# Two derivative tensors no longer stored, and the opening's x load, memsets and weight transposes moved in a four-layer forward and backward kernel

## The chip, the cores and the metric

The kernel runs on one core of a Trainium2 chip. The metric is the time of one execution in device microseconds (us); less is better.

## The reference

Input: x (2048 tokens of D = 640, bfloat16), the weights wqkv (640 x 1920) and wo (640 x 640) of a block A and of a block B, and grad_out. Four layers run, A, B, A, B, each with a residual:

```python
    x = x + _A_ref(_layernorm(x, axis=-1), A_wqkv, A_wo)
    x = x + _B_ref(_layernorm(x, axis=-1), B_wqkv, B_wo)
    x = x + _A_ref(_layernorm(x, axis=-1), A_wqkv, A_wo)
    x = x + _B_ref(_layernorm(x, axis=-1), B_wqkv, B_wo)
```

B is causal softmax attention in a window of 256 tokens, 32 heads of 20 elements. A is linear attention over all tokens with the same heads:

```python
    phi = lambda t: jnp.where(t > 0, t + 1, jnp.exp(t)) + 1e-6
    pq, pk = phi(q), phi(k)
    kv = jnp.einsum("bhsd,bhse->bhde", pk, v)
    z = jnp.einsum("bhsd->bhd", pk)
    num = jnp.einsum("bhqd,bhde->bhqe", pq, kv)
    den = jnp.einsum("bhqd,bhd->bhq", pq, z)[..., None] + 1e-6
    o = num / den
```

The kernel returns the last x and, from grad_out, the gradients of x and of the four weights. The backward pass of A needs the derivative of phi at q and at k: 1 where the argument is positive, exp(t) where it isn't, which is min(exp(t), 1). The kernel calls these eq and ek.

## The kernel before

**Tiles and stages.** The 2048 tokens are 16 tiles of 128 rows. The stages follow one another:

1. The opening (some 0 to 120 us): layer norm, q, k, v and phi of layer 0 for each tile; beside it the weights are loaded, constants are filled, and the transposed weights for the backward pass are made.
2. `a_kv(0)`: the sums over tokens of layer 0.
3. `ab_pass(0, False)`: tile by tile the end of layer 0, all of layer 1 (attention B), and layer norm with k, v of layer 2. The q work of layer 2 (`late_q`) follows, then `a_kv(2)` and `ab_pass(2, True)` (layers 2 and 3).
4. Backward: attention of layer 3, then a first pass over the tiles that ends layer 3 and does layer 2 (`lin_grads`, near 1240 to 1400 us), attention of layer 1, a second such pass (near 1960 to 2070 us), and a last part for layer 0's input.

**The opening, tile by tile.** `ln` has DVE make statistics (L476, L478), ACT form 1/sqrt (L479, L481), and DVE normalise into `hn` (L482); PE transposes `hn` (L464), ACT copies the result to `hnTA` (L467), and SP stores `hn` to DRAM for the backward pass. There is one buffer for `hn` here, so the next tile's L482 waits for PE's transposes and for this store. `a_qkv` then does six chunks of 320 columns, two for each of q, k and v, five matmuls each (L448). For q and k, ACT takes exp(t) into `ee` (L516), DVE cuts that at 1 (L517), which makes `ee` the derivative, and DVE forms phi = max(t, 1e-6) + `ee` (L520) into `pp` or `pk`. For v, ACT and DVE copy (L501, L504). phi(q) is transposed by PE and copied by ACT (`pqT`, L467). Five stores of 160 KB a tile leave on the ACT queue: pq, eq, pk, ek and v. `ee` has 4 buffers, `pp` 2.

**What stands beside it.**
- Layer 0's weight `Wqkv_A` comes in two loads on the ACT queue (chunks 0 and 1, then 2 to 5); x comes in three loads on SP (tile 0; tiles 1 to 3; tiles 4 to 15).
- `load_w`: fifteen row blocks of `Wo_A`, `Wqkv_B` and `Wo_B` on SP.
- `flip_w`: twenty times a DMA transpose of a 128 x 640 piece of a weight into one of two buffer rings (`KT`, `e`) and a DMA store of that to DRAM (`WqTB`, `WoTA`), all issued by SP. The backward passes read them.
- `zeros`: DVE memsets of `mbd`, the `qk_slab`s and the `v_slab`s (L1059), needed by later stages.
- `mask_steps`: small POOL operations.

**What sets the order.** A list scheduler (`Sched`) has each engine's instructions as operations with a planned duration, the keys they read and write, and a rank. `items` gives each piece a due time in tiles (4.5 is half a tile after tile 4 begins); the pieces are put in by due time, and `order()` then simulates the engines with the planned times and fixes each engine's own order. A key that the plan waits for, like `("rs", 0, 5)`, sets the planned place; the semaphores on the chip come from the data alone. A DMA's planned cost goes by its kind: "D" plain, "T" transposing, "B" a fixed time. On the chip SP issues its DMAs in its planned order, one behind the other: what stands behind a store that waits for its data waits too.

**The backward pass.** `lin_grads(tt)` in `start` loads for its tile, on SP, the transposed dN, pk and v, and eq and ek (two buffers each). `chunk` multiplies PE's result by eq or ek on DVE into `dqkv` (L1503). Around it in the same pass: POOL forms gw (L1327) and then, in the first pass, prod (L1377); DVE forms gcar from gw (L1329); ACT drains PE's result into dh (L1309).

Of the kernel before, what the change touches and what calls it, by code (L numbers as in the profile page):

```python
# [10 lines left out]
ACT = mybir.ActivationFunctionType  # L11
ALU = mybir.AluOpType
AX = mybir.AxisListType
BF = mybir.dt.bfloat16
# [72 lines left out]
class Sched:  # L87
# [38 lines left out]
    def order(self):  # L126
# [23 lines left out]
        while len(out) < len(self.ops):  # L150
# [16 lines left out]
            if o.dma:  # L167
                kind, size = o.dma
                if kind == "B":
                    free[e], chan_ = t + 1300, t + 2500  # L170
                elif kind == "T":
                    free[e] = t + 1100 + size / 1000
                    chan = max(chan, t + 800) + size / 140
                else:
                    free[e] = t + (330 if e == "SP" else 200)
                    chan = max(chan, t) + size / 300
                o.end = (chan_ if kind == "B" else chan) + 2000
            else:
                free[e] = t + o.dur
                o.end = free[e] + (170 if e == "PE" else 0)  # L180
# [22 lines left out]
class Kern:  # L203
    def __init__(self, ctx, tc, x0, A_wqkv, A_wo, B_wqkv, B_wo, grad_out, outs):
# [68 lines left out]
        for l in (0, 2):  # L273
            self.sv[l] = dict(
                pq=d.tile([T, D], BF, name=f"pq{l}"), pk=d.tile([T, D], BF, name=f"pk{l}"),
                eq=d.tile([T, D], BF, name=f"eq{l}"), ek=d.tile([T, D], BF, name=f"ek{l}"),
                v=d.tile([T, D], BF, name=f"v{l}"), o=d.tile([T, D], BF, name=f"o{l}"),
                r32=d.tile([T, self.H], F32, name=f"r32{l}"),
                mbd=d.tile([D, D + P], BF, name=f"mbd{l}"),
            )  # L280
# [53 lines left out]
    def forward(self, slabs):  # L334
# [5 lines left out]
        with ExitStack() as st:  # L340
# [130 lines left out]
            def ln(l, tt, hn, hnT, how):  # L471
# [13 lines left out]
                turn(how, lambda: hnT.t, lambda: hn.t, DT, [hn], [key_of(hnT)])  # L485
                dma("SP", lambda: self.tm_view(self.hn_d[l])[:, tt, :], lambda: hn.t, 160 * KB, [hn], [])

            def a_qkv(l, tt, hnT):
# [3 lines left out]
                def chunk(ci):  # L492
                    def f():
# [29 lines left out]
                        if ci == 3 and "q" in c:  # L523
                            p_, e = c["p"], c["q"]
                            turn("s", lambda: pqT[:, :, tt * P:(tt + 1) * P], lambda: p_.t, DT, [(p_, 0), (p_, 1)],
                                 [("pqT", tt)])
                            dma("ACT", lambda: self.tm_view(sv["pq"])[:, tt, :], lambda: p_.t, 160 * KB,
                                [(p_, 0), (p_, 1)], [])
                            dma("ACT", lambda e=e: self.tm_view(sv["eq"])[:, tt, :], lambda e=e: e.t, 160 * KB,
                                [(e, 0), (e, 1)], [])  # L530
                        if ci == 3:
                            e = c["k"]
                            dma("ACT", lambda: self.tm_view(sv["pk"])[:, tt, :], lambda: pk[:, tt, :], 160 * KB,
                                [("pk", tt, 2), ("pk", tt, 3)], [])
                            dma("ACT", lambda e=e: self.tm_view(sv["ek"])[:, tt, :], lambda e=e: e.t, 160 * KB,
                                [(e, 2), (e, 3)], [])
                    return f
# [4 lines left out]
            def late_q(l, tt, where="s1", **F):  # L542
# [25 lines left out]
                dma("ACT", lambda: self.tm_view(sv["pq"])[:, tt, :], lambda: p_.t, 160 * KB, [(p_, 0), (p_, 1)], [], **F)  # L568
                dma("ACT", lambda: self.tm_view(sv["eq"])[:, tt, :], lambda: e.t, 160 * KB, [(e, 0), (e, 1)], [], **F)

# [384 lines left out]
            for c0, c1 in ((0, 2), (2, 6)):  # L955
                dma("ACT", lambda c0=c0, c1=c1: wsb["Wqkv_A"][:, :, c0 * CW:c1 * CW],
                    lambda c0=c0, c1=c1: wA[:, :, c0 * CW:c1 * CW], 400 * (c1 - c0) * KB, [],
                    [("Wqkv_A", ci) for ci in range(c0, c1)])
            for t0, t1 in ((0, 1), (1, 4), (4, TT)):
                dma("SP", lambda t0=t0, t1=t1: x[:, t0:t1, :], lambda t0=t0, t1=t1: xin[:, t0:t1, :],  # L960
                    160 * (t1 - t0) * KB, [("Wqkv_A", 0)] if t0 == 4 else [], [("x", i) for i in range(t0, t1)])

# [21 lines left out]
            def ab_pass(l, last):  # L984
# [67 lines left out]
                else:  # L1052
# [3 lines left out]
            items = []  # L1056
            a_first(items, 0, 0)
            spread(items, 1.0, 9.0, [lambda f=f: op("POOL", 350, f, [], ["masks"]) for f in self.mask_steps])
            spread(items, 2.0, 12.0, [lambda t=t, v=v, n=n: op("DVE", 100 + n * 0.45, lambda: nc.vector.memset(t, v), [],  # L1059
                                                               ["zeros"]) for t, v, n in zeros])  # L1060
            for i, (k, src) in enumerate((("Wo_A", self.A_wo), ("Wqkv_B", self.B_wqkv), ("Wo_B", self.B_wo))):
                for j in range(DT):
                    tt = 1 + 3 * i + j
                    items.append((tt + 0.9, len(items), lambda k=k, src=src, j=j, tt=tt: load_w(k, src, "SP", j, [("vv", tt, 5)])))
            for i in range(4 * DT):
                at = 4.5 + 0.5 * i
                items.append((at, len(items), flip_w(i, ("rs", 0, int(at) - 1))))
            run(items)
# [22 lines left out]
    def bwd_phase(self, lb, la, nb, ahead, raw):  # L1091
# [9 lines left out]
        with ExitStack() as st:  # L1101
# [363 lines left out]
            def lin_grads(tt, items, t0):  # L1465
# [4 lines left out]
                def start():  # L1470
                    for nm, src, size in (("dNT", self.tmp_dN, 192 * KB), ("pkT", sv["pk"], 160 * KB),
# [3 lines left out]
                             [("dNd", tt)] if nm == "dNT" else [], [b])  # L1475
                    c["eq"], c["ek"] = load("eq", sv["eq"], tt), load("ek", sv["ek"], tt)

# [415 lines left out]
```

## Time and profile before

| | before |
|---|---|
| median of 3 runs | 2146.77 us (2145.37 to 2151.33) |
| the profiled execution | 2145.22 us |
| its span | 2143.5 us, so 1.7 us lie around it |
| mean granted TensorE clock | 0.975 |
| busy: PE, PEld, DVE, ACT, POOL | 2008.2, 1389.2, 1440.1, 1203.3, 879.4 us |
| DMA packets | 943687, 376.43 MB |
| eq stored from `ee` / ek stored from `ee` | 32 / 32 stores of 160 KB on the ACT queue |

PE is TensorE's matmuls, PEld its weight loads (they overlap), DVE VectorE, ACT ScalarE, POOL GpSimd, SP SyncE; SPq and ACTq are the DMA issues of an engine. A row of the list of groups names line, engine, operation, output <- inputs, shapes and count, then busy us and the mean ns of one, then idle time ahead of it and what ended that. In a timeline row stand the start, the duration, the instruction, and in brackets the idle time before it with its releaser. L-numbers are lines of the kernel before.

### The profile page before, as it was taken

To read this page: it belongs to the slowest core of one execution; us is meant where nothing else is said; L and a number is where in the kernel's file an instruction comes from. 1 tells how busy PE (TensorE), PEld (TensorE's weight loads), DVE (VectorE), ACT (ScalarE), POOL (GpSimd) and SP (SyncE) were. 2 spreads that over 40 slices of the span, in tenths; PEclk is the share of its full clock that TensorE was granted. 3 is DMA by queue.
4 is the path that set the end of the run, shared out by engine and by line. 5 is a ranking of instruction groups with operands and counts; after the bars stand their busy time and mean duration, and the time that the engine had idled before them with its cause. 6 is when DMAs were issued, how large, how long until landed. Compare 5 with 4: busy or idle time off the path is not lost. (4 is left out here: it accounts for less than half of the span.)

```text
span 2143.5 us, 68024 instructions
## 1 busy us (share of the span) xinstructions
PE 2008.2 (94%) x27908; PEld 1389.2 (65%) x27908; DVE 1440.1 (67%) x2954; ACT 1203.3 (56%) x1995; POOL 879.4 (41%) x1850
## 2 busy tenths in 40 slices
PE   6879999889999899999899999999999999999999
PEld 4656666656666577777666667656777765666764
DVE  6757777567776599999634368606998984444651
ACT  3527878647888589899422233216988881221430
POOL 1015666316777456666223223204665652230210
PEclk9989999999999899999899999999999999999999
DMA  9928989469998788987987899847999998989943
GB/s 291 256 106 179 191 193 191 119 198 201 210 208 191 146 157 151 161 161 155 193 185 168 213 200 203 175 104 142 157 158 151 170 170 162 199 185 227 186 111 102
DMA packets 943687, 376.43 MB, mean 176 GB/s; under 512 B 821776, under 2 KB 923664, under 8 KB 943120
## 3 DMA queue, kind: packets, MB, share of 16 engines
q1 hardware_dynamic: 866176, 299.16, 71.9%
q10 hardware_dynamic: 77200, 72.94, 11.1%
q8 instruction: 218, 3.57, 0.7%
q14 instruction: 93, 0.76, 0.1%
HBM read 109.02 MB, written 112.07 MB: 103 GB/s over the span
## 5 line engine op out<-in xcount | busy, mean ns | idle before, releaser
L1693 DVE TENSOR_TENSOR ds_sb<-pair,e_sb 128x768 bf16<-128x768 f32 x480 | 437.6, 951 | 57.8 <-PE pair L1654 49.6
L1673 ACT ACTIVATE e_sb<-pair 128x768 bf16<-128x768 f32 x480 | 390.9, 815 | 95.6 <-PE pair L1654 67.4
L839 POOL TENSOR_SCALAR_AFFINE_SELECT e_sb<-e_sb 128x384 bf16<-128x384 bf16 (+1 forms) x512 | 198.3, 406 | 357.5 <-ACT e_sb L830 335.7
L830 ACT ACTIVATE e_sb<-s_ps 128x1152 bf16<-128x1152 f32 (+2 forms) x256 | 273.8, 1070 | 100.2 <-PE s_ps L826 78.4
L1685 POOL TENSOR_SCALAR_AFFINE_SELECT e_sb<-e_sb 128x256 bf16<-128x256 bf16 x448 | 182.0, 406 | 227.1 <-ACT e_sb L1673 226.9
L1327 POOL TENSOR_TENSOR gw<-w,gcar 128x640 f32<-128x640 f32 x64 | 89.4, 1397 | 423.4 <-ACT w L1324 406.8
L1138 PEld LDWEIGHTS <-slabR 128*128 128x128 bf16 x1920 | 185.6, 98 | 116.1 <-DMA slabR<-o 3.7
L1682 POOL TENSOR_SCALAR_AFFINE_SELECT e_sb<-e_sb 128x256 bf16<-128x256 bf16 x512 | 206.5, 406 | 89.3 <-ACT e_sb L1673 89.3
L1718 PEld LDWEIGHTS <-dsT 128*128 128x128 bf16 x2880 | 146.2, 97 | 97.7 <-issue 91.5
L1709 ACT COPY dsT<-dsT_ps 128x768 bf16<-128x768 bf16 x240 | 191.2, 796 | 9.4 <-PE dsT_ps L1706 6.6
L448 PE MATMUL mm_ps<-slabR,hnTB 128*128 128x320 bf16 x960 | 170.5, 308 | 10.5 <-DVE gcar L520 6.0
L1706 PE MATMUL dsT_ps<-ident,ds_sb 128*128 128x128 bf16 x1848 | 158.2, 223 | 1.3 <-ACT dsT L1709 1.1
L1722 PEld LDWEIGHTS <-ds_sb 128*128 128x128 bf16 x2880 | 145.1, 96 | 0.8 <-issue 0.8
L1722 PEld LDWEIGHTS <-e_sb 128*128 128x128 bf16 x2880 | 145.0, 96 | 0.0
L844 POOL TENSOR_SCALAR_AFFINE_SELECT e_sb<-e_sb 128x512 bf16<-128x512 bf16 x224 | 142.6, 636 | 0.0
L833 ACT ACTIVATE e_sb<-s_ps 128x384 bf16<-128x384 f32 (+2 forms) x256 | 119.9, 468 | 32.3 <-PE s_ps L826 15.1
L1138 PE MATMUL dw_ps<-dqkv,slabR 128*128 128x480 bf16 x640 | 134.7, 366 | 0.0
L1309 ACT ACTIVATE dh<-mm_ps 128x320 f32<-128x320 f32 x64 | 28.0, 437 | 189.8 <-PE mm_ps L1138 164.9
L1138 PE MATMUL dw_ps<-dqkv,om 128*128 128x480 bf16 x640 | 134.2, 366 | 0.0
L1654 PE MATMUL pair<-slabR 32*128 32x384 bf16 (+2 forms) x1024 | 120.5, 326 | 12.0 <-DVE ds_sb L1693 5.2
L1138 PEld LDWEIGHTS <-om 128*128 128x128 bf16 x800 | 77.5, 98 | 71.3 <-DMA om<-o 2.4
L864 PEld LDWEIGHTS <-e_sb 128*128 128x128 bf16 x2880 | 105.5, 96 | 26.6 <-POOL e_sb L844 7.5
(234 smaller groups left out, 4357.6 us busy)
## 6 DMA issues: line engine op xcount, KB each, us to landing
qkvp<-qk_slab SPq DMA_DIRECT2D x64, 256.0 KB, 3.7
hn<-slabR SPq DMA_DIRECT2D x64, 160.0 KB, 2.9
qkvp<-v_slab SPq DMA_DIRECT2D x32, 256.0 KB, 3.4
slabR<-qkvp SPq DMA_DIRECT2D x16, 512.0 KB, 4.8
o<-o SPq DMA_DIRECT2D x48, 160.0 KB, 2.9
eq<-ee ACTq DMA_DIRECT2D x32, 160.0 KB, 3.0
pq<-pp ACTq DMA_DIRECT2D x32, 160.0 KB, 2.4
ek<-ee ACTq DMA_DIRECT2D x32, 160.0 KB, 2.7
```

Of the source, the lines that this page charges most:

```text
L448: nc.tensor.matmul(ps.t[:, w0:w0 + width], lhsT=lhsT(), rhs=rhs(), start=start, stop=stop)
L830: op("ACT", av(3 * nkt * P), lambda: nc.scalar.activation(e.t[:, 0:3, 0:nkt, :], s3.t[:, :, 0:nkt * P].rearrange("p h (i q) -> p h i q", q=P),
L839: nc.gpsimd.affine_select(out=v, in_=v, compare_op=ALU.is_ge, fill=0.0, base=0, pattern=[[0, h1 - h0], [1, P]], channel_multiplier=-1)
L1138: nc.tensor.matmul(ps.t[:, w0:w0 + width], lhsT=lhsT(), rhs=rhs(), start=start, stop=stop)
L1673: nc.scalar.activation(E[n][:, 2 * p:2 * p + 2], PR[h][:, :, 0:3 * P].rearrange("p i (j q) -> p i j q", q=P), ACT.Exp, scale=self.c_att)
L1682: nc.gpsimd.affine_select(out=e[:, :, j, :], in_=e[:, :, j, :], compare_op=ALU.is_ge, fill=0.0, base=0, pattern=[[0, 2], [-1, P]], channel ...
L1685: nc.gpsimd.affine_select(out=e[:, :, j, :], in_=e[:, :, j, :], compare_op=ALU.is_ge, fill=0.0, base=-1, pattern=[[0, 2], [1, P]], channel ...
L1693: nc.vector.tensor_mul(DS[n][:, hs], PR.pop(h)[:, :, 0:3 * P].rearrange("p i (j q) -> p i j q", q=P), E[n][:, hs])
L1706: nc.tensor.transpose(ps[:, i, j, :], DS[n][:, 2 * p + i, j, :], self.ident)
L1709: (nc.scalar.copy if by == "A" else nc.vector.tensor_copy)(TSB[h], TPS.pop(h))
L1718: nc.tensor.matmul(a[:, 0, hh, :], lhsT=TSB[2 * n + hh // 2][:, hh % 2, j, :], rhs=ld[g]["K"][:, k, cs], start=(i == 0), stop=(i == len(dq ...
L1722: nc.tensor.matmul(a[:, 1 + x, hh, :], lhsT=src[n][:, hh, j, :], rhs=ld[g][rhs][:, q, cs], start=(i == 0), stop=(i == len(dkv) - 1))
```

## The change

- **The derivative stores go.** The DRAM tensors eq and ek are gone, with their 64 stores: 32 in the opening (two a tile), 16 of ek in `ab_pass(0, False)`, 16 of eq in `late_q`. The backward pass loads pq and pk in their place and POOL forms min(phi - 1e-6, 1) in the buffer, 64 new operations of 128 x 640 bfloat16 with a planned 1000 ns.
- **The x load of tiles 4 to 15** comes at 0.5 and is planned behind tile 0's `hn` store (new key `("hnd", 0, 0)`); tile 0 and tiles 1 to 3 as before.
- **The fifteen weight loads** are keyed to the `hn` store of their tile instead of to the last copy of v of that tile.
- **The memsets** are spread from 3.0 to 13.0, each keyed to the statistics of tile 3 + 10 i / n, instead of from 2.0 to 12.0 without a key.
- **The twenty flips** are planned from 6.0 + 0.5 i instead of 4.5 + 0.5 i, each behind the statistics of the tile before.
- **The planner** gets a kind "L", with the landing time given, for the opening's large loads.

In each engine's order: SP issues the large x load right behind tile 0's `hn` store, then about one weight load a tile over tiles 1 to 14 (before: three a tile at the start); the first flip stands behind tile 4's `hn` store (before: tile 1's), the last behind tile 15's (before: tile 13's). On DVE the first large memset is the 24th instruction, and about one a tile follows to tile 13; before, they stood ahead of tile 0's statistics. The statistics and L482 of tile 1 now stand ahead of tile 0's L517. On POOL, in the steady part of the first backward pass, the order is eq's operation, gw, prod, ek's operation; in the second gw, ek's, eq's. PE has the same instructions; in `ab_pass(0, False)` a few transfers and exps change places.

```diff
+                if kind == "L":
+                    free[e], chan_ = t + 500, size - 2000
...
-                eq=d.tile([T, D], BF, name=f"eq{l}"), ek=d.tile([T, D], BF, name=f"ek{l}"),
...
-                dma("SP", lambda: self.tm_view(self.hn_d[l])[:, tt, :], lambda: hn.t, 160 * KB, [hn], [])
+                dma("SP", lambda: self.tm_view(self.hn_d[l])[:, tt, :], lambda: hn.t, 160 * KB, [hn], [("hnd", l, tt)])
...
-                            dma("ACT", lambda e=e: self.tm_view(sv["eq"])[:, tt, :], lambda e=e: e.t, 160 * KB,
-                                [(e, 0), (e, 1)], [])
...
-                            dma("ACT", lambda e=e: self.tm_view(sv["ek"])[:, tt, :], lambda e=e: e.t, 160 * KB,
-                                [(e, 2), (e, 3)], [])
...
-                dma("ACT", lambda: self.tm_view(sv["eq"])[:, tt, :], lambda: e.t, 160 * KB, [(e, 0), (e, 1)], [], **F)
...
-            for t0, t1 in ((0, 1), (1, 4), (4, TT)):
-                dma("SP", lambda t0=t0, t1=t1: x[:, t0:t1, :], lambda t0=t0, t1=t1: xin[:, t0:t1, :],
-                    160 * (t1 - t0) * KB, [("Wqkv_A", 0)] if t0 == 4 else [], [("x", i) for i in range(t0, t1)])
+                S.ops[-1].dma = ("L", 9500 if c0 else 5000)
+
+            def load_x(t0, t1, lands):
+                dma("SP", lambda: x[:, t0:t1, :], lambda: xin[:, t0:t1, :], 160 * (t1 - t0) * KB,
+                    [("hnd", 0, 0)] if t0 >= 4 else [], [("x", i) for i in range(t0, t1)])
+                S.ops[-1].dma = ("L", lands)
+            load_x(0, 1, 2800)
+            load_x(1, 4, 5500)
...
+            items.append((0.5, len(items), lambda: load_x(4, TT, 14000)))
...
-            spread(items, 2.0, 12.0, [lambda t=t, v=v, n=n: op("DVE", 100 + n * 0.45, lambda: nc.vector.memset(t, v), [],
-                                                               ["zeros"]) for t, v, n in zeros])
+            spread(items, 3.0, 13.0, [lambda t=t, v=v, n=n, i=i: op(
+                "DVE", 100 + n * 0.45, lambda: nc.vector.memset(t, v), [("rs", 0, 3 + i * 10 // len(zeros))], ["zeros"])
+                for i, (t, v, n) in enumerate(zeros)])
...
-                    items.append((tt + 0.9, len(items), lambda k=k, src=src, j=j, tt=tt: load_w(k, src, "SP", j, [("vv", tt, 5)])))
+                    items.append((tt + 0.9, len(items), lambda k=k, src=src, j=j, tt=tt: load_w(k, src, "SP", j, [("hnd", 0, tt)])))
...
-                at = 4.5 + 0.5 * i
-                items.append((at, len(items), flip_w(i, ("rs", 0, int(at) - 1))))
+                at = 6.0 + 0.5 * i
+                items.append((at, len(items), flip_w(i, ("rs", 0, min(int(at) - 1, TT - 1)))))
...
-                    c["eq"], c["ek"] = load("eq", sv["eq"], tt), load("ek", sv["ek"], tt)
+                    for nm, p_ in (("eq", "pq"), ("ek", "pk")):
+                        c[nm] = b = load(nm, sv[p_], tt)
+                        op("POOL", 1000, lambda b=b: nc.gpsimd.tensor_scalar(
+                            out=b.t, in0=b.t, scalar1=-1e-6, scalar2=1.0, op0=ALU.add, op1=ALU.min), [], [b])
```

## The prediction before the run

> **What bounds the kernel now.** First the page: the line of busy times, and the groups that price the new and the dropped work.
>
> ```profile
> span 2143.5 us, 68024 instructions
> ...
> PE 2008.2 (94%) x27908; PEld 1389.2 (65%) x27908; DVE 1440.1 (67%) x2954; ACT 1203.3 (56%) x1995; POOL 879.4 (41%) x1850
> ...
> q10 hardware_dynamic: 77200, 72.94, 11.1%
> ...
> L1327 POOL TENSOR_TENSOR gw<-w,gcar 128x640 f32<-128x640 f32 x64 | 89.4, 1397 | 423.4 <-ACT w L1324 406.8
> ...
> L844 POOL TENSOR_SCALAR_AFFINE_SELECT e_sb<-e_sb 128x512 bf16<-128x512 bf16 x224 | 142.6, 636 | 0.0
> ...
> eq<-ee ACTq DMA_DIRECT2D x32, 160.0 KB, 3.0
> ```
>
> PE is busy for 94% of the span, so 2143.5 - 2008.2 = 135 us are the most that an unchanged amount of PE work can give back. The view of busy time by stretches says where these lie (columns: stretch, length, busy us of PE, PEld, DVE, ACT, POOL, then granted clock, DMA share, GB/s).
>
> ```profile
> 0.00:25.00 25.00, 10.68 (x50) 6.37 (x51) 17.46 (x48) 6.88 (x16) 5.89 (x26) 0.88 0.94 316
> 25.00:50.00 25.00, 20.03 (x166) 14.02 (x165) 14.42 (x42) 11.75 (x30) 0.00 (x0) 0.91 0.97 279
> 50.00:75.00 25.00, 22.43 (x204) 16.43 (x203) 20.76 (x60) 16.15 (x39) 0.00 (x0) 1.00 0.90 246
> 75.00:100.00 25.00, 20.95 (x192) 15.30 (x191) 16.98 (x49) 14.68 (x38) 0.00 (x0) 1.00 1.05 263
> 100.00:125.00 25.00, 20.33 (x215) 15.37 (x213) 14.89 (x47) 9.94 (x23) 0.00 (x0) 1.00 0.63 195
> 300.00:400.00 100.00, 92.11 (x1647) 64.74 (x1645) 71.73 (x180) 81.83 (x133) 66.51 (x146) 1.00 0.83 178
> 2000.00:2020.00 20.00, 20.00 (x208) 15.85 (x206) 14.21 (x34) 8.46 (x23) 4.19 (x3) 1.00 0.84 188
> ```
>
> The first 100 us, the opening, hold 100 - (10.68 + 20.03 + 22.43 + 20.95) = 26 us of idle PE, with the DMA engines at 0.90 to 1.05. The forward pass has 8% idle beside an ACT at 82%; the last backward pass has none. So the opening is where this change can win much. Its waits (engine and line that waited <- engine and line that ended the wait: us in total, times, longest), the first row from 0 to 30 us, the others from 30 to 119:
>
> ```profile
> PE s_ps L464 <- DVE slabR L482: 13.5, 2, 9.8
> ```
>
> ```profile
> DVE ee L517 <- ACT ee L516: 17.5, 14, 3.1
> ...
> ACT hnTA L467 <- DVE pp L520: 6.2, 10, 1.2
> ...
> PE s_ps L448 <- ACT vv L501: 4.4, 7, 1.1
> ...
> PE s_ps L464 <- ACT ee L516: 3.4, 5, 1.0
> ```
>
> At first PE waits for the normalised tile (L482) of tiles 0 and 1. Later PE, DVE and ACT pass the wait round, and ACT is most often what the others wait for. The stores of the normalised tiles on SP mark the pace (start, duration):
>
> ```profile
> 20.08 0.33 SPq L416 DMA_DIRECT2D hn<-slabR  x1
> ...
> 42.50 0.33 SPq L416 DMA_DIRECT2D hn<-slabR  x1
> ...
> 50.15 0.35 SPq L416 DMA_DIRECT2D hn<-slabR  x1
> ...
> 109.62 0.34 SPq L416 DMA_DIRECT2D hn<-slabR  x1
> ```
>
> These are tiles 1, 4, 5 and 15: (42.50 - 20.08) / 3 = 7.5 us a tile early, and (109.62 - 50.15) / 10 = 5.95 us from tile 5 on.
>
> **Part 1: the memsets leave the head, the large loads move.** DVE before:
>
> ```profile
> 2.33 1.66 DVE L1059 MEMSET mbd<- 128x1920 uint32 x1 [0.35 <-issue]
> 4.04 1.57 DVE L1059 MEMSET qk_slab<- 128x512 uint32 x3
> 5.66 2.11 DVE L1059 MEMSET v_slab<- 128x512 uint32 x4
> 7.68 0.82 DVE L476 BATCH_NORM_STATS2 st<-x 128x6 f32<-128x320 bf16 x2
> ...
> 19.62 0.43 DVE L482 TENSOR_SCALAR slabR<-x,mv,rs 128x640 bf16<-128x640 bf16 x1
> ```
>
> Three groups, 1.66 + 1.57 + 2.11 = 5.3 us, stand ahead of tile 0's statistics at 7.68. In the changed order these follow the small constants, and the first large memset comes only as DVE's 24th instruction. Tile 0's x was asked for at 0.8, so its statistics can begin near 4, 3.7 us earlier. Tile 1's statistics and normalisation stand ahead of tile 0's phi work, so 19.62 can fall to about 11. PE can't use all of that, because the weights of chunks 2 to 5 must land:
>
> ```profile
> Wqkv_A<-in_A_wqkv_dram ACTq DMA_DIRECT2D x1, 1600.0 KB, 12.2
> x<-in_A_x_dram SPq DMA_DIRECT2D x1, 1920.0 KB, 15.4
> ```
>
> Asked for near 1 us and 12.2 us to landing, they arrive at 13 or 14; with the 1920 KB of x now queued behind tile 0's store, hence asked for at 6 rather than 3.4, perhaps a little earlier. From that point tile 1 follows without the gap. I take -4 us, between 0 (the loads decide) and -9 (all of 19.62 - 11). The memsets return at about one a tile, 5.3 us over ten tiles on a DVE that is busy for (20.76 + 16.98) / 50 = 75% there: nothing, +3 at most.
>
> **Part 2: 32 stores fewer in the opening.** Two things go: DMA work and ACT issue time. Queue 10 takes 11.1% of 2143.5 us for 72.94 MB, which is 0.53 us of all 16 engines for 160 KB, so 32 stores are 17 us. The five rows above from 0 to 125 us hold 25 x (0.94 + 0.97 + 0.90 + 1.05 + 0.63) = 112 us of DMA work; 95 stay. The issues, with tile 7 as the sample, and the place where ACT stood behind its own queue:
>
> ```profile
> 62.53 0.33 ACTq L416 DMA_DIRECT2D pq<-pp  x1
> ...
> 63.13 0.33 ACTq L416 DMA_DIRECT2D eq<-ee  x1
> ...
> 63.87 0.33 ACTq L416 DMA_DIRECT2D ek<-ee  x1
> ...
> 64.40 0.34 ACTq L416 DMA_DIRECT2D pk<-gcar  x1
> ...
> 65.05 0.34 ACTq L416 DMA_DIRECT2D v<-vv  x1
> ```
>
> ```profile
> 39.96 0.34 ACTq L416 DMA_DIRECT2D v<-vv  x1
> 40.35 0.44 ACT L516 ACTIVATE ee<-s_ps 128x320 bf16<-128x320 f32 x1 [2.18 <-DMA slabR<-in_B_wqkv_dram]
> ```
>
> Tiles 1 to 4: ACT's exp at 40.35 came 2.18 us late because the v store ahead of it waited for an earlier transfer, while the engines ran at 0.97. With 8 stores less (4 us of DMA work) and the 15 weight loads spread to a tile each, I take -4, between 0 (the other 1920 + 1600 KB still fill the engines) and -10 (three tiles at 5.4 instead of 7.5, and tile 4's extra wait).
>
> Tiles 5 to 15: ACT computes (16.15 + 14.68) / 50 = 62% of 5.95 = 3.7 us a tile and issues for 5 x 0.334 = 1.7, together 5.4 of 5.95. PE is busy for (22.43 + 20.95) / 50 = 87%, 5.2 us a tile, and can't go below that. Two issues less are 0.67; 5.95 - 0.67 = 5.28 is just above PE's floor. As DVE waits move into the gap, I take 0.5 a tile, 10 tiles, -5; the ends are 0 and -7.5 (PE's floor). What is late next is PE itself.
>
> The Trainium skill ("DMA: Bandwidth & Descriptors", Issuing engines are not separate DMA queues) says that an issue elsewhere saves only the sequencer's time, usually small beside the DMA. The rows agree on the size (0.33 beside 3.0 us to landing). By that rule the issue time would be worth nothing and these terms would shrink to the DMA work alone, which is the first rival's time.
>
> **Part 3: twenty flips from tile 6 on.** SP takes them in order between the stores of the normalised tiles: ten now stand among tiles 11 to 15. A flip's issue is 1 to 2 us of SP, two a tile with their stores 4 us, under the 5.4 of a tile. Nothing reads their result before the backward passes. I take 0, between -2 (early tiles freer) and +5 (one tile's pace at the end, if a late store holds the single hn buffer).
>
> **Part 4: behind the opening.** 16 ek stores leave the forward pass and 16 eq stores the q work behind it: 16 x 0.33 = 5 us of ACT issues where PE has 8% idle. Taken -2; ends -5 and +4 (the planner swaps a few transfers and exps there).
>
> **Part 5: 64 new POOL operations, 32 a pass.** None of this form (128x640 bf16 with one input) is in the trace; the nearest rows are L844 (0.64 for 512 columns, by width 0.80 for 640) and L1327 (1.40). I take 0.8. POOL is idle for most of a tile, so its time costs nothing by itself. The loads are issued a tile ahead; only the first tile may be some 0.4 late. But POOL and DVE collide. DVE, POOL, PE and ACT in the first backward pass:
>
> ```profile
> 1253.51 0.89 DVE L1329 SCALAR_TENSOR_TENSOR gcar<-slabR,sm,gw 128x640 bf16<-128x640 bf16 x1 [1.68 <-POOL gw L1327]
> 1258.85 1.95 DVE L1329 SCALAR_TENSOR_TENSOR gcar<-slabR,sm,gw 128x640 bf16<-128x640 bf16 x1 [0.35 <-POOL gw L1327]
> ```
>
> ```profile
> 1258.78 1.34 POOL L1377 TENSOR_TENSOR prod<-slab,o 128x640 f32<-128x640 bf16 x1
> ```
>
> ```profile
> 1297.85 0.44 ACT L1309 ACTIVATE dh<-dw_ps 128x320 f32<-128x320 f32 x1 [2.01 <-DVE dqkv L1503]
> ```
>
> ```profile
> 1298.43 0.42 PE L1145 MATMUL dw_ps<-slabA,pkT 128*128 128x320 bf16 x3 [0.27 <-ACT dh L1309]
> ```
>
> L1329 takes 0.89 alone and 1.95 when prod starts just before it. PE already waits 0.27 there for an ACT that waits for DVE, so DVE has no slack. The ek operation stands right behind prod on POOL. Does it hold DVE a second time? L1329 ended at 1260.80; less its own 0.89 it got going at 1259.91, 1.13 after prod began and 0.21 before prod ended. So DVE had come in before POOL's next instruction could, and I take +1 (first tiles) for the pass, with +20 as the far end. In the second pass the ek operation follows gw directly, where L1329 starts too; PE is at 20.00 of 20 and DVE at 14.21, so 0.6 a tile is covered: 0, at most +8.
>
> The Trainium skill ("GPSIMD Engine Reference", 1. Specifications) says that POOL shares its SBUF interfaces with VectorE and contends with DVE instructions of two SBUF inputs. The trace agrees (1.95 against 0.89), and the rule speaks against these 64 operations; by it the sum would be the last rival's.
>
> **Sum.** -4 - 4 - 5 + 0 - 2 + 1 = -14. The profiled run took 2145.22 us (its span and 1.7 around it), 1.6 under the median of the three; 2145.2 - 14 = 2131.
>
> **Rivals.**
> - *The opening is bound by what it moves or by PE, not by ACT.* For it: 0.90 to 1.05 DMA share, PE at 22.43 of 25. Against it: those shares include the dropped stores. Then only the head (-4) and half of the early tiles (-2) come: about 2139.
> - *The opening gives all its idle time.* Head -9, early tiles -9, later -7: with the rest about 2119. For it: 26 us of idle PE. Against it: the 12.2 us of the weights.
> - *Slower: the port in the first backward pass.* The ek operation gets the port ahead of the waiting L1329, in each steady tile, with no slack behind it. At 0.8 to 1.4 us for 14 tiles that is +11 to +20; with an opening that gives only 5 the time is 2151 to 2160, say 2155. It decides once the loss a tile passes gain / 14, 1 us by my sum. Against it: the 0.21 us just worked out.
> - *The change does nothing:* idle time goes to the next wait, 2145.
>
> **How the numbers follow.** Chances: forecast 0.53, first rival 0.18, all idle time 0.13, slower 0.09, nothing 0.07. Predicted: 2131. About 0.3% (6.4 us) is what a measurement of this kernel can tell from no change, so faster means under 2140.3. The forecast lies there nearly whole (0.51), the second rival whole, the first with more than half (0.11): 0.75. Within: 0.02 + 0.07 + 0.06 = 0.15, with 0.01 from the slower rival 0.16; slower 0.09. The range is 2112 to 2149: 2145 - 9 - 10 - 7.5 - 2 - 5 = 2112 is every term at its better end, and 2149 is the nothing case with part 4 at its worse end (+4); it leaves out the slower rival.
>
> **What would show it.** Right: tile 0's statistics near 4 us, tile 15's normalised store before 100 instead of at 109.62, 4.9 to 5.5 us a tile from tile 5 on, PE above 23 of 25 in the third stretch, L1329 still 1.95. Wrong: a store on SP held behind flips in tiles 11 to 15; L1329 at 2.7 or more; PE idle in the forward pass by what the opening gained.

## The result and the profile after

The changed kernel takes 2173.9 us (median of 4 runs, 2167.47 to 2174.88) beside 2146.07 us for the kernel before on the same chip: a ratio of 1.0124, 95% interval 1.0091 to 1.0156. It is 28 us slower. The forecast was 2131, and the range ended at 2149.

The page of the changed kernel, its line of busy times, the queue of the dropped stores, and the chain that ended last (by engine):

```profile
span 2173.2 us, 67954 instructions
...
PE 2019.4 (93%) x27908; PEld 1392.1 (64%) x27908; DVE 1440.3 (66%) x2954; ACT 1204.2 (55%) x1995; POOL 1041.4 (48%) x1914
...
q10 hardware_dynamic: 67984, 62.45, 9.3%
...
PE 5%; POOL 2%; DMA 1%; issue 1%; DVE 1%; SPq 0%; ACT 0%; ACTq 0%; POOLq 0%; DVEq 0%
```

The stores did go: queue 10 moves 62.45 MB instead of 72.94. But POOL is busy for 162 us more (1041.4 - 879.4), 2.5 us for each of the 64 new operations, and it stands in the last chain with 2%, where before it had 0%. The view of busy time by stretches, same columns and same stretches as before:

```profile
0.00:25.00 25.00, 13.45 (x82) 8.52 (x83) 13.81 (x38) 9.76 (x23) 6.01 (x26) 1.00 0.77 265
25.00:50.00 25.00, 23.45 (x208) 17.12 (x207) 20.71 (x61) 16.05 (x40) 0.00 (x0) 1.00 0.80 212
50.00:75.00 25.00, 20.15 (x193) 14.63 (x192) 19.41 (x59) 13.92 (x34) 0.00 (x0) 1.00 1.12 277
75.00:100.00 25.00, 20.68 (x173) 14.56 (x171) 16.24 (x49) 14.10 (x36) 0.00 (x0) 0.93 0.94 221
100.00:125.00 25.00, 18.18 (x183) 13.08 (x181) 13.70 (x42) 6.65 (x16) 0.00 (x0) 0.93 0.39 126
...
300.00:400.00 100.00, 91.44 (x1550) 62.48 (x1548) 70.06 (x173) 77.96 (x127) 62.81 (x139) 0.98 0.75 161
```

The first two stretches won 6.2 us of PE work (13.45 + 23.45 against 10.68 + 20.03), the third lost 2.3 (20.15 against 22.43), with the DMA engines at 1.12. The stores of the normalised tiles 1, 5 and 15 on SP (start, duration):

```profile
12.21 0.33 SPq L417 DMA_DIRECT2D hn<-slabR  x1
...
37.15 0.34 SPq L417 DMA_DIRECT2D hn<-slabR  x1
...
102.92 0.34 SPq L417 DMA_DIRECT2D hn<-slabR  x1
```

So the opening is 13.0 us ahead at tile 5 (50.15 before) and 6.7 at tile 15 (109.62). From then on the kernel falls behind. The starts of marked SP instructions in the profiled executions, with three runs explained further down, show where (us; the mbd store ends the opening, dNT is loaded once a tile in each backward pass):

| | before | after | drop_fused | drop_open | fused |
|---|---|---|---|---|---|
| hn store of tile 5 | 50.15 | 37.15 | 45.80 | 37.12 | 37.10 |
| mbd store | 121.63 | 116.25 | 113.40 | 113.65 | 115.81 |
| 24th hn store | 203.48 | 198.07 | 195.12 | 195.72 | 194.73 |
| 43rd hn store | 361.59 | 364.46 | 351.82 | 352.31 | 363.34 |
| 1st dNT load | 1083.73 | 1094.29 | 1075.96 | 1077.07 | 1088.27 |
| 16th dNT load (ends the first pass) | 1339.29 | 1355.23 | 1330.85 | 1335.23 | 1342.51 |
| 19th dNT load (second pass) | 1948.21 | 1967.91 | 1944.05 | 1944.65 | 1954.59 |
| 32nd dNT load | 2049.50 | 2077.02 | 2044.85 | 2045.82 | 2055.02 |

Against before, after is 5.4 us ahead at the mbd store and at the 24th hn store, 2.9 behind at the 43rd, 10.6 at the first dNT load, 15.9 at the 16th, 19.7 at the 19th and 27.5 at the last. Two places lose: the forward pass between the 24th and the 43rd store (8.3 us), and the backward passes. Most of the 7.7 us between the 43rd hn store and the first dNT load belongs to the backward side: the first of the new POOL operations stand there, from 1074.04 us on.

Theory P says that the backward loss is the POOL operations, by their length. Theory F says that the forward loss comes from the planner: without the stores in its account it writes another order. Rivals are late loads, the moved flips and weight loads, and the lighter ACT queue.

### The profile page after: what moved, and what is told of

Read it like the earlier page. It is cut to its first block, busy times and chain, and to the rows that moved or that the text cites. A ratio compares the mean times of both kernels' runs of the same rounds, so it can differ in the third digit from the quotient of the medians.

```text
span 2173.2 us, 67954 instructions
## 1 busy us (share of the span) xinstructions
PE 2019.4 (93%) x27908; PEld 1392.1 (64%) x27908; DVE 1440.3 (66%) x2954; ACT 1204.2 (55%) x1995; POOL 1041.4 (48%) x1914
## 3 DMA queue, kind: packets, MB, share of 16 engines
q10 hardware_dynamic: 67984, 62.45, 9.3%
## 5 line engine op out<-in xcount | busy, mean ns | idle before, releaser
L1329 POOL TENSOR_TENSOR gw<-w,gcar 128x640 f32<-128x640 f32 x64 | 89.4, 1397 | 227.8 <-ACT w L1326 214.3
L859 PE MATMUL pv_ps<-v_slab,e_sb 128*128 128x32 bf16 x2880 | 117.4, 177 | 9.3 <-POOL e_sb L839 8.3
```

The lines of the kernel that those rows point to most:

```text
L859: nc.tensor.matmul(pv.t[:, h % 16, :], lhsT=e.t[:, hh, j, :], rhs=vts[j].t[:, h, :], start=(j == 0), stop=(j == nkt - 1))
```

## The experiments

Where a run drops stores but says that the planner still counts them, each store is replaced by an operation that issues nothing and has the same planned cost:

```diff
-                            dma("ACT", lambda e=e: self.tm_view(sv["eq"])[:, tt, :], lambda e=e: e.t, 160 * KB,
-                                [(e, 0), (e, 1)], [])
+                            op("ACT", 60, lambda: None, [(e, 0), (e, 1)], [], dma=("D", 160 * KB))
```

The cut inside DVE's multiply, called the fused cut below, replaces the POOL operation:

```diff
-                            op("DVE", dve_ns(CW), lambda: nc.vector.tensor_mul(dst(), ps.t[:, 0:CW], e.t[:, e0:e0 + CW]),
+                            op("DVE", dve_ns(CW), lambda: nc.vector.scalar_tensor_tensor(
+                                out=dst(), in0=e.t[:, e0:e0 + CW], scalar=1.0, in1=ps.t[:, 0:CW], op0=ALU.min, op1=ALU.mult),
```

| run | stores | opening | order behind it | cut | median us | ratio to before (95%) |
|---|---|---|---|---|---|---|
| fused | dropped | new | new | fused | 2151.97 | 1.0032 (1.0014 to 1.0051) |
| drop_pool | dropped | old | old | POOL | 2158.65 | 1.0060 (1.0041 to 1.0079) |
| drop_fused | dropped | old | old | fused | 2134.78 | 0.9960 (0.9945 to 0.9975) |
| open_only | kept | new | old | none | 2148.77 | 1.0021 (1.0005 to 1.0036) |
| drop_open | dropped | new | old | fused | 2134.68 | 0.9946 (0.9931 to 0.9962) |
| drop_open_f45 | dropped | new, flips at 4.5 | old | fused | 2136.76 | 0.9965 (0.9952 to 0.9979) |
| drop_f60 | dropped | old, flips at 6.0 | old | fused | 2138.21 | 0.9972 (0.9956 to 0.9987) |
| drop_head | dropped | memsets and x new | old | fused | 2136.60 | 0.9962 (0.9947 to 0.9978) |
| forms | dropped | old | old | POOL, other forms | 2146.35 | 1.0003 (0.9987 to 1.0019) |
| drop_dve | dropped | new | old | DVE | 2134.02 | 0.9956 (0.9934 to 0.9979) |
| drop_f16 | dropped | new, flips at 16.0 | old | fused | 2140.24 | 0.9981 (0.9968 to 0.9994) |
| hidden | kept | new | new | none | 2176.00 | 1.0126 (1.0088 to 1.0163) |

The kernel before, measured beside each of these runs, had medians of 2144.79 to 2150.43 us, so a difference of 2 or 3 us between two rows is read from the ratios and their intervals.

**fused.** The changed kernel with the fused cut and without the POOL operations.

> The changed kernel without its 64 POOL operations: the cut min(phi, 1) is done inside DVE's existing multiply by the derivative (one instruction for one; the subtraction of 1e-6 is left out). Theory P (POOL): the operations, 2.35 to 3.04 us each in the trace, cost the 24 us that the backward passes lost (first tiles 7, first pass 8, second pass 9), so the time falls by 22 to 27 to 2147 to 2152, and the backward part is as long as before. Rival L (loads): the loads of pq and pk or the moved order of SP are late; then the backward part stays 15 us or more longer and the time is over 2160.

Measured 2151.97: 21.9 less than the changed kernel, as theory P said. In the table of marks, after minus fused is 6.0 us at the first dNT load, 12.7 at the 16th, 13.3 at the 19th and 22.0 at the last: the difference comes where the operations stand, 6 us at the first of them and the rest in the two passes. Rival L (late loads) falls, since the loads are the same here.

**drop_pool.** The kernel before without the stores, its order kept, with the POOL operations.

> The kernel before with the 64 stores dropped and the 64 POOL operations, but with the old opening and the old order of all engines in the forward pass (the planner still counts each dropped store, nothing is issued). Theory P: +24 in the backward part, 0 to -5 from the stores, so 2165 to 2171. Rival O (the opening's moves cost the time further on): 2142 to 2150.

2158.65, which is 23.9 over drop_fused: the operations' price once more, on another opening. It missed its expected range downwards because the stores are worth more than the 0 to 5 that I had put in.

**drop_fused.** The stores alone.

> The kernel before with the 64 stores dropped, every engine's order unchanged (the planner still counts them), and the cut at 1 inside DVE's multiply (without the subtraction of 1e-6): the stores alone. By the prediction's part 2 the opening's tiles go from 5.95 to 5.4 us and the early ones gain some 4, so -9 to -11 with part 4: 2135 to 2138. If stores hide behind other work: within 3 of 2146.

2134.78, 10.9 under the 2145.63 of before beside it. The marks are 8.2 us ahead at the mbd store and 9.8 at the 43rd hn store; 7.8 are left at the first dNT load and 4.7 at the last, in a profiled execution of 2140.33 us, above the run's median. Part 2 of the prediction (with 2 for part 4) had this size.

**open_only.** The opening's moves with all stores kept, and the old order behind.

> The changed kernel's opening (x load, memsets, weight loads, flips) with all 64 stores kept and the old backward pass; the order behind the opening is that of the kernel before. Theory F (the forward pass lost its 10 us because the planner, not seeing the stores, ordered its DMAs and exps otherwise): the opening's gain, 0 to 7, stays to the end, 2139 to 2146. Rival: the moved flips and loads cost it, and the forward pass is 5 to 10 longer here too, 2146 to 2156.

2148.77, 3 us slower than before, which misses theory F's range and lies in the rival's. But the place isn't the rival's: the mbd store comes at 126.4 instead of 121.63, and from there on the lag stays at 4.7 us to the 43rd hn store (366.33 against 361.59). So the order of before doesn't lose time in the forward pass, as theory F has it, and the new opening is no gain while the stores stand.

**drop_open.** drop_fused with the new opening; it differs from fused only in that the planner counts the stores.

> The stores alone (the run drop_fused) plus the whole changed opening; the planner still counts the dropped stores, so the order of every engine behind the opening is that of the kernel before. It differs from the run fused in the planner's view alone. Theory F (in fused the planner, not seeing the stores, put the forward pass in an order that lost 10 us): nothing is lost between tiles 7 and 16 of the forward pass, and the time is 2152 - 10 to 13 = 2139 to 2142. Rival C (a lighter ACT queue or the new opening slows the forward pass whatever the order): it is lost here too, 2150 to 2153.

2134.68, 17.3 under fused (18 by the ratios), beyond the 10 to 13 expected; rival C falls. The profiled executions show less of it: fused is 11.0 us later at the 43rd hn store and 9.5 at the end, but drop_open's was its slowest of ten, 2141.32. Busy time from 200 to 350 us, first of drop_open, then of fused:

```profile
200.00:350.00 150.00, 143.07 (x2483) 101.08 (x2482) 116.77 (x291) 124.18 (x201) 99.56 (x219) 1.00 0.88 181
```

```profile
200.00:350.00 150.00, 136.37 (x2292) 94.36 (x2290) 107.30 (x267) 113.62 (x187) 91.60 (x202) 0.99 0.81 168
```

PE does 6.7 us less in fused, with the lighter queue in both. What the new order waits for, by fused's list of waits for the same stretch (us in total, times, longest):

```profile
DVE qk_slab L690 <- PE mm_ps L449: 21.1, 19, 3.4
...
ACT e_sb L825 <- PE mm_ps L449: 15.5, 8, 2.3
```

The first kind of wait in drop_open's list:

```profile
DVE qk_slab L695 <- PE mm_ps L449: 7.3, 17, 0.9
```

ACT in the changed kernel, which has the new order too:

```profile
261.53 1.13 ACT L825 ACTIVATE e_sb<-s_ps 128x1152 bf16<-128x1152 f32 x1 [2.30 <-PE mm_ps L449]
...
278.75 1.13 ACT L825 ACTIVATE e_sb<-s_ps 128x1152 bf16<-128x1152 f32 x1 [1.83 <-PE mm_ps L449]
```

About once a tile ACT's exp now stands idle for some 2 us until a projection of PE has ended; drop_open's list has none of this kind among its twelve largest. In that order SP transposes `oTB` four instructions earlier, PE starts more of the q, k, v chunks in halves with scores between them, DVE's copies and norm steps shift with them, and ACT issues the `o` and `linv` stores ahead of an exp. So more changes in each tile than the few transfers and exps of the section on the change. Which of these swaps costs most wasn't tried.

**hidden.** The crossing's fourth corner: stores issued, planner not told.

```diff
+                            S.ops[-1].dma, S.ops[-1].dur = None, 0
```

(behind each of the eq and ek stores of open_only.)

> The other half of the crossing: the changed opening with all 64 stores issued and the old backward pass (the run open_only), but the planner is not told of the eq and ek stores, so PE, DVE, POOL and SP have the order of the run fused. Order and stores are then crossed: order of before and stores dropped 2134.7, order of before and stores issued 2148.8, new order and stores dropped 2152.0. Theory F (the new order costs 17 by itself): 2160 to 2168, and PE is busy for some 136 to 138 of the 150 us from 200 to 350, as in fused. Rival C (only the lighter ACT queue under that order loses time; with the stores issued it is harmless): 2146 to 2152.

2176.00, 27 over open_only, but before had 2150.43 beside it and 2145.63 beside open_only; by the two ratios it is 1.0126 - 1.0021, 22 us. In the profiled executions 3.6 us of it are there at the 24th hn store and 20.3 at the 43rd. Its own row from 200 to 350 us:

```profile
200.00:350.00 150.00, 135.85 (x2216) 91.76 (x2213) 104.24 (x260) 110.89 (x180) 89.49 (x195) 0.97 0.78 170
```

The new order costs 17 with the stores dropped and 22 with them issued, more than the 11 to 19 that I expected. Theory F is shown: the order alone does it, whether the stores are there or not. Why it costs more with the stores wasn't tried; the granted clock is 0.97 in this row and 0.99 in fused's.

**drop_open_f45, drop_f60, drop_head.** Pieces of the opening, all without the stores and with the old order behind.

> As drop_open, but the twenty flips at their old due times 4.5 + 0.5 i and old keys. Theory D (flips due at 6.0 leave the DMA engines idle at 20 to 40 us, 0.56 to 0.70 busy in the trace, and crowd them behind, over 1.0, so the 12 us that the head wins are lost again): tile 15's store comes 5 to 10 earlier than with 6.0, 2130 to 2135. Rival W (the weight loads, one a tile, or the memsets lose it): as drop_open within 3.

> As drop_fused, with the flips alone moved to 6.0 + 0.5 i. Theory D: some 5 slower than drop_fused, 2138 to 2142. Rival W: within 3 of 2135.

> As drop_fused, with the memsets and the x load of the changed kernel, but flips and weight loads keyed as before. Theory D: it keeps the head's gain, 5 to 12 below drop_fused, 2123 to 2130. Rival (the 112 us of DMA work bound the opening whatever the order): within 3 of 2135.

They took 2136.76, 2138.21 and 2136.60, with mbd stores at 114.0, 113.9 and 115.5; drop_fused has 113.40 and drop_open 113.65. So neither the flips' due time nor the head decides the end of the opening, and theory D falls, though drop_f60's number lies in its range: its 3.4 over drop_fused is within overlapping intervals. The hn store of tile 5 came at 36.40, 44.83 and 44.01 (drop_fused 45.80, drop_open 37.12). drop_open_f45 and drop_head differ in the weight loads alone, so the lead of some 9 us at tile 5 needs the new places of the weight loads; the memsets and the x load give 2 of it. That lead is gone by the end in every run that has it.

**drop_f16.** The flips leave the tiles' stretch.

```diff
-                at = 6.0 + 0.5 * i
+                at = 16.0 + 0.5 * i
```

> As drop_open, with the twenty flips due at 16.0 + 0.5 i, behind the opening's tiles. All openings without the 64 stores so far have tile 15's store near 101 us whatever was moved. Theory M (the opening is bound by the DMA work in it, some 95 us): 20 flips with their stores, some 25 us of DMA work, leave it, so tile 15's store comes 8 or more earlier, under 94; the total falls by 5 or more to under 2130 unless SP then holds up the forward pass. Rival E (the engines' chain in each tile bounds it): tile 15's store stays within 3 of 102.

The hn store of tile 15, by which both theories go, and busy time from 60 to 80 us, each of drop_open, then of drop_f16:

```profile
101.77 0.34 SPq L417 DMA_DIRECT2D hn<-slabR  x1
```

```profile
94.53 0.48 SPq L417 DMA_DIRECT2D hn<-slabR  x1
```

```profile
60.00:80.00 20.00, 16.51 (x139) 11.93 (x138) 13.73 (x45) 10.52 (x27) 0.00 (x0) 0.91 1.02 260
```

```profile
60.00:80.00 20.00, 18.25 (x171) 13.28 (x169) 15.87 (x52) 13.35 (x34) 0.00 (x0) 1.00 0.48 160
```

The store came 7.2 us earlier: just short of theory M's 8, and well outside theory E's 3. The DMA share fell from 1.02 to 0.48 and PE did 1.7 us more in these 20, at a granted clock of 1.00 instead of 0.91. So the DMA work seems to set part of the tiles' pace. Yet DVE began the last part of mbd at 110.5 instead of 113.4: only 2.9 us are left there for some 25 us of DMA work moved. From 100 to 120 us, where the flips now stand, the DMA share is 0.95 instead of 0.57 and PE is busy for 13.44 instead of 15.98 us. Neither theory is settled. Then SP worked through its flips from 90 to 134 us, the next tile's hn store waited for that until 135.28, and the whole took 2140.24, 5.6 over drop_open.

**forms.** Every engine's order of drop_pool, with other POOL operations: one operation for eq, and a product of two inputs for ek, which leaves the derivative at k out.

```diff
-                        op("POOL", 1000, lambda b=b: nc.gpsimd.tensor_scalar(
+                        op("POOL", 1000, lambda b=b, nm=nm: nc.gpsimd.tensor_scalar(
-                            out=b.t, in0=b.t, scalar1=-1e-6, scalar2=1.0, op0=ALU.add, op1=ALU.min), [], [b])
+                            out=b.t, in0=b.t, scalar1=1.0, scalar2=None, op0=ALU.min) if nm == "eq" else
+                            nc.gpsimd.tensor_tensor(out=b.t, in0=b.t, in1=b.t, op=ALU.mult), [], [b])
```

> As drop_pool, every engine's order unchanged, with two other forms of the POOL operation: for eq one operation (minimum with 1) in place of two, for ek a product of the buffer with itself (two inputs; ek is then not the derivative of phi at k). Theory P in its narrow form (the loss is the length of the operations): the product takes some 1.4 us like the other two-input POOL rows, the single operation less than 2.35, and the loss of 24 against drop_fused falls in proportion to what is over the slack, to 12 or less: 2137 to 2147. Rival (what costs is that POOL takes the shared port at all, or the wait for the load in POOL's order): the time stays at 2155 or more.

The groups of the new operations (line, engine, operation, shapes, count, then busy us and mean ns), first in the changed kernel, then in forms:

```profile
L1480 POOL TENSOR_SCALAR eq<-eq 128x640 bf16<-128x640 bf16 x32 | 77.9, 2433 | 19.7 <-DMA eq<-pq 9.8 <-DVE slabR L1461 6.1 <-PE dw_ps L1140 1.7
L1480 POOL TENSOR_SCALAR slabR<-slabR 128x640 bf16<-128x640 bf16 x16 | 42.8, 2673 | 17.8 <-DMA slabR<-pk 16.6
...
L1480 POOL TENSOR_SCALAR ek<-ek 128x640 bf16<-128x640 bf16 x16 | 41.8, 2615 | 26.1 <-DMA ek<-pk 22.8 <-DVE dqT L1173 1.6 <-DVE gcar L1331 1.0
```

```profile
L1475 POOL TENSOR_SCALAR eq<-eq 128x640 bf16<-128x640 bf16 x32 | 59.9, 1872 | 31.1 <-DMA eq<-pq 29.1 <-DVE sm L1317 0.9 <-DVE sm L1320 0.9
L1477 POOL TENSOR_TENSOR slabR<-slabR 128x640 bf16<-128x640 bf16 x16 | 26.2, 1635 | 17.1 <-DMA slabR<-pk 16.8 <-DVE sm L1317 0.2
...
L1477 POOL TENSOR_TENSOR ek<-ek 128x640 bf16<-128x640 bf16 x16 | 20.8, 1303 | 36.3 <-DMA ek<-pk 30.0 <-DVE sm L1317 5.4 <-DVE gcar L1326 0.9
```

The work falls from 77.9 + 42.8 + 41.8 = 162.5 us to 59.9 + 26.2 + 20.8 = 106.9, and the loss against drop_fused from 23.9 to 11.6 us (by the ratios from 21.5 to 9.2). The same number of operations, at the same places, cost half when they are a third shorter: their length is what costs, theory P in its narrow form, and the rival falls.

**drop_dve.** drop_open with the cut as an operation of its own on DVE, planned at 450 ns, with the subtraction.

> As drop_open, with the cut as an operation of its own on DVE (with the subtraction of 1e-6), 64 operations of 128x640, which by the 0.24 us of 128x320 should take 0.45 us each. DVE is 68 to 71 of 100 busy in these passes. Theory P: 32 x 0.45 = 14 us a pass lies in DVE's idle time, the time is 2135 to 2140. Rival (DVE's order puts them ahead of what PE waits for, so most of their length shows): 2145 to 2160.

2134.02: nothing over drop_open. The operations' groups, and busy time in the middle of the first backward pass and of the second, of drop_dve and then of the changed kernel:

```profile
L1485 DVE TENSOR_SCALAR eq<-eq 128x640 bf16<-128x640 bf16 x32 | 14.4, 449 | 7.5 <-DMA eq<-pq 7.5
...
L1485 DVE TENSOR_SCALAR ek<-ek 128x640 bf16<-128x640 bf16 x16 | 6.4, 398 | 13.5 <-DMA ek<-pk 13.5
...
L1485 DVE TENSOR_SCALAR slabR<-slabR 128x640 bf16<-128x640 bf16 x16 | 5.1, 316 | 0.3 <-DMA slabR<-pk 0.2
```

```profile
1255.00:1345.00 90.00, 87.72 (x804) 65.92 (x803) 85.30 (x193) 29.34 (x77) 29.56 (x22) 1.00 1.01 203
1985.00:2050.00 65.00, 65.00 (x664) 51.37 (x662) 54.36 (x129) 26.86 (x70) 13.22 (x11) 1.00 0.88 174
```

```profile
1255.00:1345.00 90.00, 81.41 (x733) 60.69 (x731) 70.26 (x150) 27.45 (x71) 74.10 (x38) 0.98 0.91 192
1985.00:2050.00 65.00, 59.13 (x573) 45.60 (x572) 38.95 (x88) 21.29 (x55) 48.72 (x23) 0.97 0.85 170
```

The same arithmetic takes DVE 0.3 to 0.45 us where POOL needs 2.4 to 2.7, and PE is busy for 87.72 of 90 and 65.00 of 65; with POOL it is 81.41 and 59.13. (The passes start at other times in the two kernels, so the stretches don't hold quite the same tiles.) drop_dve computes all that the reference asks and is faster than both kernels: 0.9956 of before (0.9934 to 0.9979). It wasn't shown to beat drop_open or drop_fused.

The way from before to after, step by step in medians: stores -10.9 (drop_fused), the new opening -0.1 (drop_open), the new order +17.3 (fused), POOL +21.9 (after), together +28.2; measured +27.8. As each step starts where the last one ends, this sum has to come out and proves nothing by itself. What bears the parts out is that each was measured a second time elsewhere: POOL +23.9 with the old opening, the order +22 with the stores, the stores -14.1 with the new opening, which alone is +3.1 with the stores (open_only). So the parts hold to some 5 us, not to a tenth.

## Why the prediction was wrong

**Part 5, the price of the POOL operation: the step that failed first.** I took 0.8 us, from L844 by width, with L1327's 1.40 as the far bound. In the sum part 5 stood at +1; it measured +21.9 (after against fused). The operation takes 2.35 us alone. Both bounds were of other kinds of instruction: a select, and a product of two inputs. The trace of before had no arithmetic of POOL with two constants, and forms shows that the kind decides: 1.30 to 1.64 for the product, 1.87 for one constant, 2.43 to 2.67 for two, all of 128x640. "POOL is idle for most of a tile, so its time costs nothing by itself" went with it: two operations with gw and prod are 2 x 2.4 + 1.4 + 1.3 = 7.5 us of an 8.3 us tile ((1339.29 - 1248.39) / 11 before), and POOL works in order. The first tiles, for which the sum had +1, show it. POOL's rows in the changed kernel, then DVE's, which waits for the last of them, and DVE's in the kernel before:

```profile
1074.04 3.04 POOL L1480 TENSOR_SCALAR eq<-eq 128x640 bf16<-128x640 bf16 x1
1077.16 2.34 POOL L1480 TENSOR_SCALAR slabR<-slabR 128x640 bf16<-128x640 bf16 x1
1079.58 2.35 POOL L1480 TENSOR_SCALAR eq<-eq 128x640 bf16<-128x640 bf16 x1
1082.01 1.39 POOL L1420 TENSOR_TENSOR prod<-slabA,o 128x640 f32<-128x640 bf16 x1
```

```profile
1083.43 0.82 DVE L1422 TENSOR_REDUCE dd<-prod 128x32 f32<-128x640 f32 x1 [6.16 <-POOL prod L1420]
```

```profile
1073.89 0.82 DVE L1420 TENSOR_REDUCE dd<-prod 128x32 f32<-128x640 f32 x1 [1.51 <-POOL prod L1418]
```

prod stands behind three cuts, and DVE waits 6.16 us for it instead of 1.51. Where the first pass proper begins, POOL and DVE in the changed kernel:

```profile
1262.81 2.35 POOL L1480 TENSOR_SCALAR slabR<-slabR 128x640 bf16<-128x640 bf16 x1
1265.24 1.39 POOL L1329 TENSOR_TENSOR gw<-w,gcar 128x640 f32<-128x640 f32 x1
1266.72 3.04 POOL L1480 TENSOR_SCALAR eq<-eq 128x640 bf16<-128x640 bf16 x1
1269.84 2.35 POOL L1480 TENSOR_SCALAR slabR<-slabR 128x640 bf16<-128x640 bf16 x1
1272.26 1.40 POOL L1329 TENSOR_TENSOR gw<-w,gcar 128x640 f32<-128x640 f32 x1
1273.62 1.34 POOL L1379 TENSOR_TENSOR prod<-slab,o 128x640 f32<-128x640 bf16 x1
1275.05 2.80 POOL L1480 TENSOR_SCALAR eq<-eq 128x640 bf16<-128x640 bf16 x1
```

```profile
1273.69 1.95 DVE L1331 SCALAR_TENSOR_TENSOR gcar<-slabR,sm,gw 128x640 bf16<-128x640 bf16 x1 [2.04 <-POOL gw L1329]
```

From 1262.81 to 1277.85 POOL has no gap over 0.1 us. Before, each gw but the first stood behind 4.0 to 7.0 us of idle time in this pass and waited for ACT alone; now these stand behind two cuts in POOL's order, and DVE waits 2.04 us for gw. That is a first tile. DVE's waits for POOL in the whole first pass (us in total, times, longest), of before, then of the changed kernel:

```profile
DVE gcar L1329 <- POOL gw L1327: 10.3, 16, 2.5
```

```profile
DVE gcar L1331 <- POOL gw L1329: 11.2, 16, 2.5
...
DVE dqkv L1508 <- POOL slabR L1480: 7.0, 10, 1.5
```

In the first pass the wait for gw is thus hardly longer in sum; what is new is that the multiply waits for the cut itself. In the second pass two cuts and gw are 2 x 2.35 + 1.4 = 6.1 us of the 6.6 that a tile took before ((2034.56 - 1995.10) / 6 by the starts of gw), and DVE waits for gw in 13 of the 16 tiles instead of 3. The same wait of before, then of the changed kernel:

```profile
DVE gcar L1329 <- POOL gw L1327: 4.1, 3, 2.5
```

```profile
DVE gcar L1331 <- POOL gw L1329: 21.0, 13, 3.8
```

For the second pass the sum had 0, at most 8; the marks give 8.7 between the 19th and the last dNT load (after minus fused, 13.3 to 22.0).

**The slower rival was right in its sign and wrong in its place.** It had the ek operation hold the port against L1329. The row above has L1331 (the old L1329) at 1.95 as before, with eq's operation queued right behind prod: DVE came in first, as worked out from the 0.21 us. All of DVE's work is no longer than before (1440.3 against 1440.1 us busy). What lost the time was POOL's own queue. I had named that queue nowhere as a bound.

**Part 4, the planner's swaps: mis-sized.** I allowed +4 for "a few transfers and exps"; they cost 17.3 us (drop_open against fused), and PE's and DVE's orders were among what changed. The diff of the orders was in my hands, and I judged it by its number of lines, not by who would wait in it.

**Part 2, the stores: right in size.** -9 with -2 of part 4 was forecast, -10.9 measured alone. By tile the terms hold too: drop_fused is 4.35 us ahead at tile 5 and takes (101.39 - 45.80) / 10 = 5.56 us a tile from there, 0.39 less than before where 0.5 was taken. But the early -4 counted on the weight loads as well, which drop_fused leaves alone, so that it fits so closely is in part luck. Whether the DMA work or ACT's issue time is what the stores cost was not separated.

**Part 1, the head: right at its place, worth nothing at the end.** The statistics of tile 0 began at 3.47 us (near 4 was worked out) and tile 1's store came at 12.21 (11 for its L482). At tile 5 that was 13 us with the stores and the weight loads. But tiles 5 to 15 then took (102.92 - 37.15) / 10 = 6.6 us each, not 4.9 to 5.5, and PE had 20.15 of 25 in the third stretch, not 23. drop_open and drop_fused end the opening within 0.3 us of one another. The first rival (bound by what it moves or by PE) said so. Two comparisons speak for what it moves: with the new opening the 32 stores bring tile 15's store from 101.77 to 114.35 (drop_open, open_only), and the flips' leaving brings it to 94.53 (drop_f16). But of the latter's 7.2 us only 2.9 are left at the last part of mbd. What bounds the opening's second half stays open.

**Part 3, the flips: right** that their due time is worth about nothing by itself.

## What to carry to other kernels

Price a new instruction by a row of the same kind on the same engine, and when there is none, let the range hold a cost several times the nearest row; then add it to everything that engine already does in the tile, in its order, before calling it idle time. Removing an operation also removes it from the planner's account: keep its planned cost as an empty operation to see what the removal is worth and what the new order costs, for here the order took back more than the removal gave. A head start at the beginning of a stage is worth only what is left of it at the stage's end.

## What the runs showed of the hardware

- POOL with two constants on 128x640 bf16 took 2.35 us alone, DVE 0.32 to 0.45 (means) for the same.
- What the prediction called the port costs POOL too: its operation took 3.04 us where L1331 ran beside it, and L1331 then kept its 0.88:

```profile
1281.88 0.88 DVE L1331 SCALAR_TENSOR_TENSOR gcar<-slabR,sm,gw 128x640 bf16<-128x640 bf16 x1 [0.36 <-POOL gw L1329]
```

```profile
1281.93 3.04 POOL L1480 TENSOR_SCALAR slabR<-slabR 128x640 bf16<-128x640 bf16 x1
```

Whoever came first ran at its own length here: POOL's operation began 0.05 us later and took 0.7 longer; beside prod it was DVE that came 0.07 us later and took 1.1 longer (the row at 1273.69).
